# An attention and feed-forward kernel: the head's loads in 2 KB packets, its mask on VectorE, and the scores by chunks of keys

## The chip, the cores and the metric

The kernel runs on one core of a Trainium2 chip. The metric is the device time of one execution in microseconds (us); lower is better. The kernel was already tuned: TensorE is busy for 98% of the time, and a change of one microsecond is a third of a per cent. Executions of the same kernel spread over about 1 us.

## The reference

```python
# q, k, v: 8 batches x 8 heads x 576 positions x 64; w_in 512x2048, w_out 2048x512
scores = scale * np.matmul(q, k.transpose(0, 1, 3, 2))
mask = np.abs(pos[:, None] - pos[None, :]) <= 32          # a band
scores = np.where(mask, scores, -1000000000.0)
attn = softmax(scores)                                    # (max taken off, divided by the sum)
x = np.matmul(attn, v)            # -> 4608 tokens x 512
h = x @ w_in
g = h * (1.0 / (1.0 + np.exp(-1.702 * h)))
out = g @ w_out
```

## The kernel before

The tokens of all batches go through in 36 units of 128 keys. A unit has scores (TensorE), exponential (ScalarE), the band mask, values (TensorE), a normalisation (VectorE) and a transpose of x (TensorE in the head, by DMA later). Two units give 256 tokens for layer 1 and layer 2 of the feed-forward part, which fill TensorE. One call of `layer1`, eight matmuls, is called a layer-1 block here. The change touches the head, that is, the time before TensorE is in that dense part, and the scores.

In the head, the first batch comes in two parts: positions 0 to 320 ("A") and 320 to 576 ("B"). In part B, four neighbouring positions of one head are one piece of 1 KB in float32. Two heads are first copied side by side ("pairing", on VectorE), then transposed together:

```python
self.span = {"A": (0, 320), "B": (320, 256)}
...
def pair_heads(self, c, i, hp, eng, src=None):
    ...
    self.cast(eng, self.stage[c, i, "c"][:n, hp], src.rearrange("p h (j d) -> p j h d", j=JT))
...
def head(self):
    ...
    self.setup_neg()                    # triangles of -30000, five operations on GpSimd
    for m in range(3):
        self.load_v(m)                  # GpSimd issues these loads
    for c in "kq":
        self.load_heads("B", c)
    self.load_w_in(0)
    self.load_v(3)
    self.load_v(4, 0)
    for c in range(1, 4):
        self.load_w_in(c)
    ...
    for hp in range(4):
        self.pair_heads("k", "B", hp, dve)
    for hp in range(3):
        self.pair_heads("q", "B", hp, dve)
    for hp in range(4):
        if hp == 2:
            self.blind_again(3, 0)
        self.rows_T("k", "B", hp, "htho"[hp], dve)      # transposes, then a copy out of PSUM
        if hp == 0:
            self.pair_heads("q", "B", 3, dve)
        self.rows_T("q", "B", hp, "hoth"[hp], act)
    self.scores(2)
    self.scores(3)
    self.odd_v(2, dve)
    self.odd_v(3, dve)
    self.layer1(0, 0)
    self.values(2)
    self.norm(2)
    self.layer1(0, 1)
    self.values(3)
    self.norm(3)
    self.x_T(2, "t")
    ...
```

`blind(u)` writes the triangles of -30000 into the PSUM bank of the scores (PSUM is where this kernel's matmuls write) by a matmul with the identity, so that the first units need no mask afterwards. `odd_v` makes, on VectorE, a second copy of a v tile (`vo`) that is shifted by half a tile. `keep_busy` runs matmuls on zeros ("fillers", named junk in the profile). The scores of a unit were 32 matmuls of 64 keys by 64 queries:

```python
for hp in range(4):
    for blk in range(2):
        k0, q0 = (128 * u + 64 * blk) % RING, (128 * u + 64 * blk + 32) % RING
        for half in range(2):
            lo, at = 64 * half, k0 + 64 * (half ^ blk)
            for eo in range(2):
                r = slice(eo * 64, eo * 64 + 64)
                nc.tensor.matmul(sc[eo][lo:lo + 64, 2 * hp + blk, :], self.kT[r, hp, at:at + 64],
                                 self.qT[r, hp, q0:q0 + SQ], ...)
```

The softmax here doesn't subtract the row's maximum and nothing guards it: scores larger than these inputs give would overflow.

## Time and profile before

| | before |
|---|---|
| time, median of the first three executions | 293.69 us (293.09 to 294.04) |
| span of the profiled execution | 291.3 us |
| part B's queries land | 15.15 us |
| their scores start | 17.22 us |
| first layer-1 block starts | 18.25 us |
| second quarter of w_in lands | 21.18 us |
| third layer-1 block starts (needs that quarter) | 21.23 us |
| last matmul starts | 287.66 us |

All but the first two rows are times from the span's start. The prediction below shows the page's lines, the chain of the head and the transfers. This is VectorE's timeline; the bracket is the idle time ahead and what ended it.

```profile
13.73 1.17 DVE L105 COPY kc<-ks 64x512 bf16<-64x512 bf16 x4
15.17 0.69 DVE L105 COPY qc<-qs 64x512 bf16<-64x512 bf16 x3 [0.27 <-DMA qs<-in_q_dram]
```

The chain of waits goes through the 7.28 us of that query load. But VectorE had been pairing keys until 0.27 us before its first query copy. Had the queries come earlier, it would have been ready for them only 0.27 us sooner.

### The profile page before, as it was taken

Reading aid. Unit: us, or ns where it says so; the run is one execution under the profiler, and the core shown is the slowest. Engines: PE = TensorE matmul, PEld = TensorE weight load, DVE = VectorE, ACT = ScalarE, POOL = GpSimd, SP = SyncE. Lnnn points to the kernel's source line nnn. Section 1 sums busy time; section 2 is a strip of 40 time slices with the busy share of each in tenths; the row PEclk is TensorE's granted clock in tenths of the full one; section 3 lists DMA queues with packets and bytes.
Section 4 is the critical chain, followed back from the end, with each engine's and each line's share of the span. In section 5 each row is a group of like instructions: output and inputs, shape, how many; then the busy total and the mean of one; then the engine's idle time right before and its main releaser. Section 6 shows DMA issues by size and latency. Waiting matters only on the chain.

```text
span 291.3 us, 9542 instructions
## 1 busy us (share of the span) xinstructions
PE 285.4 (98%) x4021; PEld 234.7 (81%) x4021; DVE 188.7 (65%) x556; ACT 185.0 (64%) x306; POOL 102.1 (35%) x142
## 2 busy tenths in 40 slices
PE   7999999999999999999999999999999999999995
PEld 2569765866888888888888888888888888888884
DVE  3682477678575858585858585858585858583353
ACT  4677547685766767676767676767575757575330
POOL 8945534999536442543433434332000000000000
PEclk9999999999999999999999999999999999999999
DMA  9999999999999999999999999999915330303012
GB/s 149 156 191 206 199 186 178 168 136 154 159 136 189 137 158 156 146 145 158 161 154 164 184 103 150 142 178 115 183 36 144 39 99 13 100 13 100 2 72 72
DMA packets 145291, 38.83 MB, mean 133 GB/s; under 512 B 129888, under 2 KB 140896, under 8 KB 145248
## 3 DMA queue, kind: packets, MB, share of 16 engines
q0 software_dynamic: 97696, 18.16, 88.6%
q1 hardware_dynamic: 47104, 19.67, 41.0%
q8 instruction: 31, 0.51, 0.8%
q10 hardware_dynamic: 448, 0.39, 0.5%
q14 instruction: 12, 0.10, 0.1%
HBM read 36.96 MB, written 9.44 MB: 159 GB/s over the span
## 4 chain that ended last, share of the span: by engine, by line
PE 92%; DMA 2%; POOL 2%; DVE 1%; issue 0%; ACT 0%; POOLq 0%; DVEq 0%
PE h_ps L319 43%; PE o_ps L381 32%; PE o_ps L331 7%; PE sc L251 4%; PE pv L279 4%; DMA qs<-in_q_dram 2%; PE tp L179 1%; POOL ve L160 1%; PE tp L306 0%; POOL ks L137 0%; DVE qc L105 0%; DVE o_sb L399 0%; POOL neg L219 0%; DVE kT L105 0%; POOL qs L137 0%
## 5 line engine op out<-in xcount | busy, mean ns | idle before, releaser
L319 PE MATMUL h_ps<-xT,w_in_sb 128*128 128x256 bf16 x1152 | 135.1, 273 | 0.0
L321 ACT ACTIVATE g<-h_ps 128x512 f16<-128x512 f32 x144 | 85.5, 595 | 73.4 <-PE h_ps L319 72.1
L319 PEld LDWEIGHTS <-w_in_sb 128*128 128x128 bf16 x1152 | 112.0, 98 | 13.4
L160 POOL DMA_DIRECT2D ve<-in_v_dram x40 | 34.2, 859 | 76.5 <-PE pv L279 62.9
L381 PEld LDWEIGHTS <-gs 128*128 128x128 f16 x480 | 45.8, 98 | 5.8
L381 PE MATMUL o_ps<-w_sum,gs 128*128 128x256 f16 x360 | 44.3, 273 | 0.0
L257 ACT ACTIVATE p<-sc 128x512 bf16<-128x512 f32 x72 | 37.2, 604 | 2.7 <-PE sc L251 2.5
L381 PEld LDWEIGHTS <-g 128*128 128x128 f16 x360 | 34.1, 98 | 4.6 <-ACT g L321 0.2
L358 DVE TENSOR_TENSOR gs<-g 128x512 f16<-128x512 f16 x30 | 12.7, 425 | 38.1 <-ACT g L321 38.1
L291 DVE TENSOR_TENSOR x<-pv,rec 128x256 bf16<-128x256 f32 x72 | 30.6, 425 | 2.5
L381 PE MATMUL o_ps<-w_out_sb,g 128*128 128x256 f16 x240 | 29.0, 273 | 0.0
L105 DVE COPY part<-o_ps 128x256 f32<-128x256 f32 x45 | 19.1, 424 | 12.7 <-PE o_ps L381 11.6
L399 DVE TENSOR_TENSOR o_sb<-o_ps,part 128x256 f32<-128x256 f32 x45 | 19.0, 422 | 12.0 <-PE o_ps L381 11.4
L268 DVE TENSOR_TENSOR p<-p,mask 128x512 bf16<-128x512 bf16 x64 | 24.5, 424 | 0.7 <-ACT p L257 0.7
L147 POOL DMA_DIRECT2D qs<-in_q_dram x27 | 23.0, 873 | 4.7 <-DMA ks<-in_k_dram 2.9
L105 DVE COPY vo<-ve 64x528 bf16<-64x528 bf16 x69 | 21.8, 316 | 3.8 <-DMA ve<-in_v_dram 2.3
L147 POOL DMA_DIRECT2D ks<-in_k_dram x27 | 22.7, 856 | 3.9 <-DMA ks<-in_k_dram 1.8
L331 PE MATMUL o_ps<-w_out_sb,g 128*128 128x512 f16 x96 | 23.2, 380 | 0.0
L418 ACT ACT_TABLE_LOAD x15 | 19.2, 1283 | 0.3
L257 ACT ACT_TABLE_LOAD x15 | 19.2, 1283 | 0.3
L290 DVE RECIPROCAL rec<-pv 128x4 f32<-128x4 f32 x72 | 12.6, 175 | 8.3 <-PE pv L279 8.1
L279 PEld LDWEIGHTS <-p 128*64 128x64 bf16 x576 | 11.2, 110 | 5.9 <-DVE p L268 3.6
(71 smaller groups left out, 243.3 us busy)
## 6 DMA issues: line engine op xcount, KB each, us to landing
out_dram<-o_sb SPq DMA_DIRECT2D x34, 256.0 KB, 4.5
ve<-in_v_dram POOLq DMA_DIRECT2D x32, 128.0 KB, 6.8
ks<-in_k_dram POOLq DMA_DIRECT2D x22, 128.0 KB, 10.0
qs<-in_q_dram POOLq DMA_DIRECT2D x22, 128.0 KB, 12.1
w_in_sb<-in_moe_w_in_dram POOLq DMA_DIRECT2D x4, 512.0 KB, 11.2
w_out_sb<-in_moe_w_out_dram POOLq DMA_DIRECT2D x4, 512.0 KB, 15.1
ve<-in_v_dram POOLq DMA_DIRECT2D x8, 64.0 KB, 6.7
ks<-in_k_dram POOLq DMA_DIRECT2D x7, 64.0 KB, 5.5
```

Of the source, the lines that this page charges most:

```text
L105: (eng.copy if eng is self.nc.scalar else eng.tensor_copy)(out, in_)
L147: self.nc.gpsimd.dma_start(self.stage[key][off:off + m, n], src[b, :, s:s + m, :].rearrange("h s d -> s h d"))
L160: self.nc.gpsimd.dma_start(self.ve[m % NV][off:off + n, :, :self.D], self.v[b, :, s:s + n, :].rearrange("h s d -> s h d"))
L257: nc.scalar.activation(p[:, eo], sc[eo], AF.Exp, scale=self.scale)
L268: self.nc.vector.tensor_mul(pv, pv, msk.to_broadcast([128, 4, 2, SQ]))
L279: nc.tensor.matmul(acc[half][blk * 64:blk * 64 + 64, hh, :], p[:, h % 2, h // 2 * 2 + blk, :], vt[:, h, :D + 1], start=(hh == 0), stop=(hh ...
L291: nc.vector.tensor_mul(x[:, hs, :], acc[half][:, :, :D], rec[:, hs, :].to_broadcast([128, 4, D]))
L319: nc.tensor.matmul(hps[:, i, :], self.w_in_sb[:, kr, ff * 128:(ff + 1) * 128], self.xT[t][:, kr, :], start=(i == 0 and kr == 0), stop=(i = ...
L321: nc.scalar.activation(self.g[t][:, ffs[0]:ffs[1] + 1:ffs[1] - ffs[0], :], hps, AF.Gelu_apprx_sigmoid)
L331: nc.tensor.matmul(o_ps, self.g[t][:, ff, s * 128:(s + 1) * 128], self.w_out_sb[:, ff, :], start=(ff == 0), stop=(ff == self.NFF - 1))
L381: nc.tensor.matmul(self.part[t, key], x, y, start=(first and k == 0), stop=(k == 7), skip_group_check=True)
L418: self.nc.scalar.activation(self.spark, self.spark, AF.Gelu_apprx_sigmoid)
```

## The change

The intent is to start the dense part earlier: issue the loads sooner (mask off GpSimd), land the queries sooner (2 KB pieces, half a v tile behind the first weights), and get from landing to scores without pairing copies (64 small transposes, and for each of keys and queries two copies "side by side" on VectorE and ScalarE). The scores of a unit become 24 matmuls, by three chunks of keys of which the middle one meets 128 queries. Both first layer-1 blocks now come ahead of both value units. Twelve fillers become seven.

```diff
+    def load_rest(self, c):
+        ...
+        for g in range(2):
+            self.nc.gpsimd.dma_start(rest[32 * g:32 * g + 32],
+                                     src[0, 4 * g:4 * g + 4, 320:576, :].rearrange("h (p j) d -> p h (j d)", j=8))
+
+    def rest_T(self, c, kind, engs):
+        tp = self.bank(kind, [128, 2, 8, 64], BF16, "tp")
+        for n in range(4):
+            for j in range(8):
+                self.nc.tensor.transpose(tp[64 * (n % 2):64 * (n % 2) + 64, n // 2, j, :],
+                                         self.stage[c, "B"][:64, n, j * self.D:(j + 1) * self.D], self.ident[:64, :64])
+        ...
+        for g in range(2):
+            self.cast(engs[g], dst[:, 2 * g:2 * g + 2, 320:576].rearrange("r h (p j) -> r h p j", j=8),
+                      tp[:, :, :, 32 * g:32 * g + 32].rearrange("r h j p -> r h p j"))
...
# setup_neg: one memset and four selects on GpSimd become 14 small VectorE operations
...
         for hp in range(4):
-            for blk in range(2): ...                     # 8 matmuls of 64x64 per hp, as above
+            for chunks in ((1, 0), (2,)):                # 6 matmuls per hp
+                for eo in range(2):
+                    r = slice(eo * 64, eo * 64 + 64)
+                    for c in chunks:
+                        lo = 64 * (c % 2)
+                        b0, n = (1, 1) if c == 2 else (0, 1 + c)
+                        nc.tensor.matmul(sc[eo][lo:lo + 64, 2 * hp + b0:2 * hp + b0 + n, :],
+                                         self.kT[r, hp, k0 + 64 * c:k0 + 64 * c + 64],
+                                         self.qT[r, hp, q0 + SQ * b0:q0 + SQ * (b0 + n)], ...)
...
-        for m in range(3):
+        for m in range(2):
             self.load_v(m)
-        for c in "kq":
-            self.load_heads("B", c)
+        self.load_v(2, 0, 64)
+        for c in "kq":
+            self.load_rest(c)
         self.load_w_in(0)
+        self.load_v(2, 64)
...
         self.blind(2)
+        self.rest_T("k", "t", (act, dve))
+        self.x_T(0, "h", act)
+        self.x_T(1, "h", act)
+        self.rest_T("q", "o", (dve, act))
         self.blind(3)
-        (pairing copies, 32 transposes of pairs, eight copies)
+        self.keep_busy(2, "h")
         self.scores(2)
         self.scores(3)
...
         self.layer1(0, 0)
+        self.layer1(0, 1)
         self.values(2)
         self.norm(2)
-        self.layer1(0, 1)
         self.values(3)
```

More of the change, by code (lines that the diff above doesn't have):

```diff
@@ L55, in __init__ @@
         self.stage, self.paired = {}, set()
-        self.span = {"A": (0, 320), "B": (320, 256)}
+        self.span = {"A": (0, 320)}
         self.xT, self.g, self.o_ps = {}, {}, {}
@@ L155, in rows_X, with load_v @@
                                              self.stage[c, i][:, n].rearrange("p h d -> p (h d)"))
-    def load_v(self, m, half=None):
-        for i, (off, b, s, n) in enumerate(self.pieces(128 * m, 128)):
-            if half in (None, i):
-                self.nc.gpsimd.dma_start(self.ve[m % NV][off:off + n, :, :self.D],
-                                         self.v[b, :, s:s + n, :].rearrange("h s d -> s h d"))
+    def load_v(self, m, lo=0, hi=128):
+        for off, b, s, n in self.pieces(128 * m + lo, hi - lo):
+            self.nc.gpsimd.dma_start(self.ve[m % NV][lo + off:lo + off + n, :, :self.D],
+                                     self.v[b, :, s:s + n, :].rearrange("h s d -> s h d"))
     def odd_v(self, m, eng):
@@ L191, in rows_T @@
                   tp[:, :, :size // JT].rearrange("r j p -> r p j"))
+    def load_rest(self, c):
+        rest = self.stage[c, "B"] = self.work.tile([128, 4, 8 * self.D], BF16, name=c + "s", tag=c + "s", bufs=3)
+        src = {"q": self.q, "k": self.k}[c]
+        for g in range(2):
[7 more added lines that the diff above has]
+                                         self.stage[c, "B"][:64, n, j * self.D:(j + 1) * self.D], self.ident[:64, :64])
+        dst = {"q": self.qT, "k": self.kT}[c]
+        for g in range(2):
+            self.cast(engs[g], dst[:, 2 * g:2 * g + 2, 320:576].rearrange("r h (p j) -> r h p j", j=8),
+                      tp[:, :, :, 32 * g:32 * g + 32].rearrange("r h j p -> r h p j"))
     def load_raw(self, c, hp, eng):
@@ L210, in setup_neg @@
     def setup_neg(self):
-        pool = self.nc.gpsimd
+        dve, pad = self.nc.vector, SQ // 2
+        lo, hi = slice(0, 64), slice(64, 128)
         self.neg = self.cst.tile([128, 2, SQ], BF16, name="neg")
-        pool.memset(self.neg, 0.0)
-        for b in range(2):
-            for half in range(2):
-                sign = 1 if half == b else -1
-                ap = self.neg[64 * half:64 * half + 64, b, :]
-                pool.affine_select(out=ap, in_=ap, compare_op=ALU.is_ge, fill=-30000.0, base=0,
-                                   pattern=[[-sign, SQ]], channel_multiplier=sign)
-    def blind_again(self, u, eo):
-        neg = self.neg.rearrange("k (o b) s -> k o b s", o=1).to_broadcast([128, 4, 2, SQ])
-        self.nc.tensor.matmul(self.sc[u][eo].rearrange("k (h b) s -> k h b s", b=2), self.ident, neg,
-                              start=True, stop=False, skip_group_check=True)
+        tri = [self.cst.tile([128, pad + SQ], BF16, name=f"tri{i}") for i in range(2)]
+        for i in range(2):
+            dve.memset(tri[i][:, :pad], 0.0)
+        for rows in (lo, hi):
+            dve.tensor_copy(tri[0][rows, pad:], self.ident[rows, rows])
+        for i in range(6):
+            a, b = tri[i % 2], tri[(i + 1) % 2]
+            dve.tensor_add(b[:, pad:], a[:, pad:], a[:, pad - (1 << i):pad + SQ - (1 << i)])
+        for rows, b in ((lo, 0), (hi, 1)):
+            dve.tensor_scalar(out=self.neg[rows, b, :], in0=tri[0][rows, pad - 1:pad + SQ - 1], scalar1=-30000.0,
+                              scalar2=None, op0=ALU.mult)
+            dve.tensor_scalar(out=self.neg[rows, 1 - b, :], in0=tri[0][rows, pad:], scalar1=30000.0, scalar2=-30000.0,
+                              op0=ALU.mult, op1=ALU.add)
     def blind(self, u):
@@ L241, in scores @@
         sc = self.sc.pop(u)
-        n = 0
+        k0, q0 = 128 * u % RING, (128 * u + 32) % RING
         for hp in range(4):
-            for blk in range(2):
-                k0 = (128 * u + 64 * blk) % RING
-                q0 = (128 * u + 64 * blk + 32) % RING
-                for half in range(2):
-                    lo, at = 64 * half, k0 + 64 * (half ^ blk)
-                    for eo in range(2):
-                        r = slice(eo * 64, eo * 64 + 64)
-                        nc.tensor.matmul(sc[eo][lo:lo + 64, 2 * hp + blk, :], self.kT[r, hp, at:at + 64],
-                                         self.qT[r, hp, q0:q0 + SQ], start=(seen and n == 0),
-                                         stop=(n == 7), skip_group_check=not seen)
-                n += 1
+            for chunks in ((1, 0), (2,)):
[6 more added lines that the diff above has]
+                                         self.kT[r, hp, k0 + 64 * c:k0 + 64 * c + 64],
+                                         self.qT[r, hp, q0 + SQ * b0:q0 + SQ * (b0 + n)],
+                                         start=(seen and hp == 0 and c < 2), stop=(hp == 3 and c > 0),
+                                         skip_group_check=not seen)
         p = self.work.tile([128, 2, 8, SQ], BF16, name="p", tag="p", bufs=5)
@@ L436, in head @@
         self.setup_neg()
-        for m in range(3):
+        for m in range(2):
             self.load_v(m)
+        self.load_v(2, 0, 64)
         for c in "kq":
-            self.load_heads("B", c)
+            self.load_rest(c)
         self.load_w_in(0)
+        self.load_v(2, 64)
         self.load_v(3)
-        self.load_v(4, 0)
+        self.load_v(4, 0, 64)
         for c in range(1, 4):
@@ L452, in head @@
         self.load_w_out(1)
-        self.load_v(4, 1)
+        self.load_v(4, 64)
         for m in range(5, 7):
@@ L471, in head @@
         self.odd_v(0, dve)
-        self.odd_v(1, act)
+        self.odd_v(1, dve)
         self.keep_busy(3, "h")
@@ L475, in head @@
         self.norm(0)
-        self.keep_busy(3, "o")
-        self.x_T(0, "t", act)
-        self.keep_busy(1, "o")
+        self.keep_busy(2, "o")
         self.values(1, "oa")
         self.norm(1)
-        self.keep_busy(4, "a")
-        self.x_T(1, "a", act)
         self.blind(2)
+        self.rest_T("k", "t", (act, dve))
+        self.x_T(0, "h", act)
+        self.x_T(1, "h", act)
+        self.rest_T("q", "o", (dve, act))
         self.blind(3)
-        self.keep_busy(1, "h")
-        for hp in range(4):
-            self.pair_heads("k", "B", hp, dve)
-        for hp in range(3):
-            self.pair_heads("q", "B", hp, dve)
-        for hp in range(4):
-            if hp == 2:
-                self.blind_again(3, 0)
-            self.rows_T("k", "B", hp, "htho"[hp], dve)
-            if hp == 0:
-                self.pair_heads("q", "B", 3, dve)
-            self.rows_T("q", "B", hp, "hoth"[hp], act)
+        self.keep_busy(2, "h")
         self.scores(2)
```

## The prediction

> **What bounds the kernel now.** I read the page first, then the chain of waits of the first 24 us, the DMA issues with their landings, and the timelines of GpSimd and TensorE there.
>
> ```profile
> PE 285.4 (98%) x4021; PEld 234.7 (81%) x4021; DVE 188.7 (65%) x556; ACT 185.0 (64%) x306; POOL 102.1 (35%) x142
> PE 92%; DMA 2%; POOL 2%; DVE 1%; issue 0%; ACT 0%; POOLq 0%; DVEq 0%
> ```
>
> TensorE carries 92% of the chain that ended last; everything else on it is the head. So two things can shorten the kernel: less TensorE work in the dense part, or an earlier start of it. The chain of waits shows the head (start, length, what):
>
> ```profile
> 4.37 2.85 POOL ve L160 x3
> 7.21 0.66 POOL ks L137
> 7.87 7.28 DMA qs<-in_q_dram
> 15.15 0.02 issue
> 15.17 0.69 DVE qc L105 x3
> 15.86 0.33 DVE kT L105
> ...
> 17.29 0.48 PE sc L251 x24
> 17.77 0.02 issue
> 17.79 0.53 PE sc L251 x40
> 18.32 0.98 PE h_ps L319 x8
> 19.30 0.38 PE pv L279 x16
> ```
>
> The second part of the first batch's queries is issued at 7.87 us and lands at 15.15. From there 2.07 us of copies and transposes lead to the scores at 17.22 in TensorE's timeline, and the first layer-1 block follows at 18.25. After that TensorE has no visible gap. But there is a second limit close behind. In GpSimd's timeline the second quarter of w_in is issued at 10.88, and the DMA view of that moment gives its time to landing (last column):
>
> ```profile
> 10.88 2.27 POOL L109 DMA_DIRECT2D w_in_sb<-in_moe_w_in_dram  x3
> w_in_sb<-in_moe_w_in_dram POOLq DMA_DIRECT2D x1, 512.0 KB, 10.3
> ```
>
> 10.88 + 10.3 is 21.2 us. The first block that needs that quarter is the third layer-1 block, and in TensorE's timeline it starts at 21.23:
>
> ```profile
> 21.23 1.05 PE L319 MATMUL h_ps<-xT,w_in_sb 128*128 128x256 bf16 x8
> ```
>
> So queries and weights are limits of almost equal length. If only the queries came earlier, TensorE would stand before this weight quarter instead. Later weights have room: the third quarter of w_in lands near 23.8 and is needed near 26.7.
>
> **What the Trainium skill says.** (1) "PSUM — Partial Sum Buffer", section "PSUM bank collisions raise a hardware error": two engines must not touch one bank and quadrant at once, reads against reads included, and ACT against DVE is made to wait as well. Each of the change's two copies "side by side" reads all 128 partitions of one 2 KB bank. In the built program's order the VectorE copy of the keys waits for ScalarE's, and ScalarE's copy of the queries waits for VectorE's. So I take them as one after the other; before, no such pair exists, so the trace can't show it. (2) "DMA: Bandwidth & Descriptors", section "Why small descriptors are slow (HBM only)": a fixed cost per packet and descriptor. The trace agrees: the old loads (512 packets with 1 KB read each) land 1.97 us apart, k at 7.20 + 6.0 = 13.2, q at 7.87 + 7.3 = 15.17; the first w_in quarter (512 packets with 2 KB read) lands 2.2 us later (8.54 + 8.8 = 17.3). Twice the bytes cost little more than the same number of packets. (3) "TensorE: Matmul & The Clock Gate", section "What's actually happening": the array's clock halves after an idle window of about 3.4 us. In the trace the first eight fillers take 3.55 us, 0.44 each, and three later ones 0.82 us together, so a gap that is too long would show.
>
> **The change part by part.**
>
> *Mask on VectorE.* GpSimd loses one memset and four selects, 2.97 to 4.32 us in its timeline: 1.35 us before the first v load. VectorE gains about 14 small operations in a chain. It sits idle 3.01 us until 4.43, waiting for the raw keys; at an estimated 0.13 us each (between its 72 ns memsets and 0.175 us reciprocals) that is 1.8 us and hidden. How much of GpSimd's 1.35 us reaches the landings? The v loads land 4.1 us after their issue at 4.32 and 5.3, about 0.97 apart, as the issues do, so they are partly limited by issue; but the loads ahead of them land only at 2.34 + 5.0 = 7.34. I count 0.3 us.
>
> *Half of a v tile behind the first w_in quarter.* The third v tile lands at about 11.35, 1.95 after the second. Half of it moved: 0.5 to 1.0 us for the queries, nothing for the second w_in quarter, which still comes after it.
>
> *2 KB packets.* Keys and queries go from 512 packets each to 256 of double size. By the w_in row, 256 such packets cost half of 2.2 to 2.55 us (the quarters of w_in land about 2.5 us apart later), so 1.1 to 1.3 us instead of about 1.9: 0.6 to 0.8 each, 1.2 to 1.6 for both. I take 1.2. This shifts everything behind, the weights too.
>
> Queries: 15.15 - 0.3 - 0.7 - 1.2 gives about 12.9. Second w_in quarter: 21.2 - 0.3 - 1.2 gives about 19.7.
>
> *From the queries' landing to the scores.* The pairing copies go (eight of 0.29 us on VectorE). Instead 32 transposes of 64 columns (one per 16 ns by the old 64-column pairs: 0.5 us, with latency 0.7), then two copies of 128x512 with a strided side. Today's rows for this form are 0.69 us on VectorE and 0.585 on ScalarE. One after the other with semaphores: 0.7 + 0.69 + 0.59 + 0.1, about 2.1 us. That is the 2.07 of before: truly parallel copies would have given 1.5. The first half of the first score unit can start after the first copy, which gains another 0.3 or so. Scores would end at 12.9 + 2.1 + 0.6, about 15.6 instead of 18.25.
>
> *Order behind the scores.* Two layer-1 blocks (0.98 each) to 17.6, then both value units (0.38 each) one after the other, to 18.4. The transposes of the first unit wait for its normalisation, two pairs of 0.18 + 0.42 us on VectorE, until about 19.1: a new stall of about 0.7 us, since a layer-1 block no longer lies between. TensorE is at the third layer-1 block at about 19.3. The weights are there at 19.7. So the weights end it: 21.2 - 19.7, a gain of 1.5 us.
>
> *Scores by key chunks.* Matmuls per unit go from 32 to 24, with the same columns. Does the count or the columns cost? The chain of waits has both kinds near each other:
>
> ```profile
> 46.77 0.38 PE pv L279 x16
> 47.15 0.38 PE sc L251 x32
> ```
>
> 16 value matmuls run two at a time, 32 scores four at a time: eight rounds each, of 64 or 65 columns, and the same 0.38 us. Rounds cost, not instructions. In the new order each head pair still sends chunks 0 and 2, 64 columns each, through the same quarter of the array, while chunk 1 with 128 columns runs beside them: eight rounds per unit again. I count 0.1 us over all 36 units, and at the very most 1 us.
>
> *Fillers.* Twelve fall to seven. All stand in times of waiting; not on the path.
>
> Sum: 1.5 + 0.1, about 1.6; I take off 0.1 for friction. 293.7 - 1.5 = 292.2 us.
>
> **The rivals.** First, the head gains its full shift of the queries, about 2.5 us, and the weights keep up: against it speaks the landing at 21.2 beside the use at 21.23. It would give 291.2. Second, the landing hardly moves: transfers of the same bytes are already at the rate of the memory, and the packets were not the cost. For it speaks that larger loads later run 1 KB reads nearly as fast (the 448 KB k load has 896 packets and lands 15.6 us after issue, in a full queue). Then only the half v tile is left, the weights do not move, and the time stays at 293.3. Third, the new stall at the transposes and serial copies, perhaps a halved clock with five fillers gone, eat it up: about 293.5 to 294. Fourth, fewer score matmuls do pay, if issue and weight loads bound them (24 for 32, a quarter of 0.25 us over 36 units, 2.3 us at most): 290. The equality of the two 0.38 us rows speaks against it.
>
> **Range and chances.** The first two rivals give 291.2 and 293.3, and runs of before spread over 0.95 us. Eight times in ten I expect 291.0 to 293.5. A change of 2% would be 5.9 us; the head has at most some 4 us to give, and no part adds as much. So within 2%: 0.97, faster 0.02, slower 0.01.
>
> **What would show it.** Right: the queries land near 12.9 us; the scores end near 15.6; TensorE waits for VectorE before the transposes after the first two layer-1 blocks; the third layer-1 block starts with the landing of the second w_in quarter, near 19.7; a steady score unit still costs 0.38 us in the chain, and the distance from that block to the end is unchanged. Wrong: a score burst that is clearly shorter (fourth rival), queries landing after 14 us (second), the two copies from one bank overlapping in time, or fillers and transposes at twice their length before the scores (the clock).

## The result, and the profile after

| | before | after | predicted |
|---|---|---|---|
| time, median of 4 executions each, us | 293.47 | 291.61 | 292.2 |
| ratio (95% interval) | | 0.9941 (0.9915 to 0.9967) | |
| part B's queries land, us | 15.15 | 12.74 | 12.9 |
| scores of part B start / first layer-1 block starts, us | 17.22 / 18.25 | 15.42 / 16.37 | – / 15.6 |
| second w_in quarter lands, us | 21.18 | 19.49 | 19.7 |
| third layer-1 block starts, us | 21.23 | 19.95 | 19.7 |
| last matmul starts, us | 287.66 | 285.89 | – |

Ratios here are the mean time of one kernel's fast runs over that of the other's of the same rounds, so they are not quite the ratio of the medians quoted. Repeated later on another chip (the last experiment), the changed kernel gave 0.9985 (0.9964 to 1.0006): the two sets put the gain at 0.6% and at 0.15%, and the second alone can't be told from no gain.

The profiled executions differ by 1.77 us at the last matmul. 1.28 us of that are there at the third layer-1 block; 0.49 come later. The page of the changed kernel, busy times and the chain by engine:

```profile
PE 282.7 (98%) x3757; PEld 233.5 (81%) x3759; DVE 192.0 (66%) x562; ACT 183.7 (63%) x302; POOL 101.8 (35%) x140
PE 94%; DMA 2%; DVE 1%; ACT 1%; issue 0%; ACTq 0%; DVEq 0%
```

TensorE has 264 matmuls fewer and is busy 2.7 us less. The chain still is TensorE's; the 2% of GpSimd on it are gone. The chain of waits through the head, after (start, length, what):

```profile
12.27 0.82 PE tp L205 x32
13.09 0.55 PE tp L326 x8
13.64 0.84 PE tp L205 x32
...
14.51 0.70 DVE qT L105
...
15.23 0.59 ACT qT L105
...
15.87 0.57 PE sc L270 x25
16.44 1.85 PE h_ps L339 x16
18.29 0.27 PE pv L299 x8
...
18.58 0.19 DVE rec L310
...
18.80 0.42 DVE x L311
19.23 0.10 DVE rec L310
...
19.35 0.43 DVE x L311
...
19.83 0.28 PE tp L326 x2
```

Three things are to be seen. No transfer stands on it: the queries land at 12.74, but TensorE comes to their transposes only at 13.64, behind the keys' transposes (12.27) and those of x (13.09). The two copies of the queries follow one another (VectorE 14.51, ScalarE 15.23), as predicted. And the third layer-1 block is held by the normalisation, from 18.56 to 19.83; the weights had been there since 19.49. For those, the lines of GpSimd's timeline and of the transfers after:

```profile
11.15 2.27 POOL L109 DMA_DIRECT2D w_in_sb<-in_moe_w_in_dram  x3
w_in_sb<-in_moe_w_in_dram POOLq DMA_DIRECT2D x1, 512.0 KB, 8.3
```

The second quarter is issued 0.27 us later than before (11.15 against 10.88) and yet lands 1.7 us earlier, for it takes 8.3 us instead of 10.3; probably less is ahead of it in the queue by then, since more had been moved before. These are the windows of 9 to 12 us of before, then after; the last number is GB/s moved, and the five pairs are the busy times of TensorE, its weight loads, VectorE, ScalarE and GpSimd:

```profile
9.00:12.00 3.00, 2.74 (x39) 1.12 (x27) 1.41 (x5) 2.95 (x6) 3.00 (x5) 1.00 1.38 143
```

```profile
9.00:12.00 3.00, 2.83 (x68) 1.48 (x56) 2.79 (x10) 2.07 (x4) 2.60 (x5) 1.00 1.25 202
```

143 GB/s become 202. In the dense part, a pair of score units in the chain, before and then after:

```profile
107.58 0.67 PE sc L251 x64
```

```profile
106.11 0.63 PE sc L270 x32
```

A pair costs 0.04 us less (the count at the end is of the matmuls that the chain goes through, of 64 and 48). A unit by itself, further up in both chains, still takes 0.38 us.

### The profile page after: what moved, and what is told of

It reads as the page before. It is cut to its first block, busy times and chain, and to the rows that moved or that the text cites.

```text
span 289.8 us, 9009 instructions
## 1 busy us (share of the span) xinstructions
PE 282.7 (98%) x3757; PEld 233.5 (81%) x3759; DVE 192.0 (66%) x562; ACT 183.7 (63%) x302; POOL 101.8 (35%) x140
## 4 chain that ended last, share of the span: by engine, by line
PE 94%; DMA 2%; DVE 1%; ACT 1%; issue 0%; ACTq 0%; DVEq 0%
PE h_ps L339 43%; PE o_ps L401 32%; PE o_ps L351 7%; PE pv L299 4%; PE sc L270 4%; DMA q_raw<-in_q_dram 2%; PE tp L178 1%; PE tp L326 1%; PE tp L205 1%; ACT qT L105 0%; ACT p L277 0%; PE sc L253 0%; DVE x L311 0%; DVE o_sb L419 0%; DVE qT L105 0%
## 5 line engine op out<-in xcount | busy, mean ns | idle before, releaser
L105 DVE COPY vo<-ve 64x528 bf16<-64x528 bf16 x71 | 24.5, 345 | 4.7 <-DMA ve<-in_v_dram 3.1
L105 DVE COPY part<-o_ps 128x256 f32<-128x256 f32 x45 | 19.1, 423 | 12.4 <-PE o_ps L401 11.4
```

The source lines that it names most:

```text
L105: (eng.copy if eng is self.nc.scalar else eng.tensor_copy)(out, in_)
```

## The experiments

The theory after the result: the loads gain from the mask, the half tile and the packets together, the pairing copies no longer stand behind them, and the steady scores give up to half a microsecond. The rivals: one of these parts gives it all, or the new stall and the serial copies keep back a gain that a small repair would release. The experiments came in three sets of four, each set on one chip with its own runs of the kernel before (medians 293.40, 293.26 and 292.97). All twelve gave the right result.

**1. The old score matmuls in the changed kernel.**

```diff
-            for chunks in ((1, 0), (2,)): ...      # 24 matmuls per unit
+            for blk in range(2): ...               # the old 32 per unit
```

> The changed kernel with the score matmuls of before (32 per unit instead of 24), nothing else. Theory: fewer instructions pay only where two units stand together (bursts of 64): 0.67 us for such a pair instead of 0.63, some 14 pairs, so about 0.5 us longer than the changed kernel, near 292.1; the third layer-1 block still starts at 19.9 to 20.0. Rival (the prediction's 0.1 us): 291.7, and the 0.04 us per pair come from something else in the changed kernel, so the pairs stay at 0.63.

Measured: 293.31 us, ratio 1.0003 (0.9970 to 1.0036). The whole gain is gone, although the queries landed at 12.92 and the second weight quarter at 20.35. Its chain of waits shows why:

```profile
13.65 0.52 PE tp L205 x18
14.16 0.94 issue
15.10 0.51 PE tp L205 x14
...
19.45 0.60 PE pv L299 x29
20.05 1.22 issue
21.27 0.22 PE pv L299 x3
```

"issue" is time in which the engine waited for nothing that the profile shows. TensorE stops for 0.94 us in the middle of 32 equal transposes, whose data had been there for 1.2 us, and for 1.22 us within the value matmuls. The first pause falls after matmul 220 of TensorE's recorded order, the second after matmul 346. In the changed kernel (runs 7 and 12 show it best, with 0.44 and 0.22 us) a pause after the same matmul (221 in traces that have one more record before it) falls behind the second blind, in time that TensorE spends waiting for the copies anyway. Sixteen more score matmuls ahead of it, eight in each of the first two units, move it into the transposes. Between the two pauses lie 127 weight loads, as many matmuls (one has no record) and two semaphore instructions: 256 instructions.

The traces also show what the pauses end with. One DMA queue moves instructions, in packets of 16 KB. Its line on the page of this run, then of the changed kernel (packets, MB, share):

```profile
q8 instruction: 32, 0.52, 0.8%
```

```profile
q8 instruction: 29, 0.48, 0.7%
```

It has three packets more where TensorE has 288 matmuls more. The times of its first packets are read from the traces:

| | packet starts, us | packet ends, us | TensorE goes on, us | from the packet's end, us |
|---|---|---|---|---|
| run 1, first pause | 12.70 | 13.64 | 15.10 | 1.46 |
| run 1, second pause | 18.82 | 19.76 | 21.27 | 1.51 |
| run 6 | 12.46 | 13.83 | 15.40 | 1.57 |
| run 10 | 13.22 | 14.25 | 15.67 | 1.42 |

Runs 7, 8 and 12 have 1.44, 1.49 and 1.44 us. So TensorE goes on 1.4 to 1.6 us after such a packet in all seven pauses, also where the packet took longer (run 6) or came later (run 10). The kernel before reaches its matmul 220 only at 17.3 us, long after its packet (12.02 to 13.17), and doesn't stop there. That TensorE waits in these pauses for its next instructions fits all of this; no run moved a packet by itself, so it isn't proved by experiment.

**2. The new score matmuls alone in the kernel before.** (The edit is the score part of the diff above.)

> The kernel before with the new score matmuls alone. Theory: the head is as before (third layer-1 block at 21.2, queries at 15.1), pairs of units take 0.63 instead of 0.67 us, and the time is about 0.5 us under before: 293.0. Rival (0.1 us): 293.4. If issue bound all scores, each unit would fall from 0.38 too, and the time by over 1 us.

Measured: 293.01 us, 0.9986 (0.9949 to 1.0023), not told apart from nothing. The scores of the dense part did take 0.66 us less, but layer 2 and the values took 0.9 us more (see run 7). The trace was worth more than the time. In this run the unchanged loads landed the queries at 13.83, 1.3 us before those of the first profile, and the weights at 20.53. Yet the scores started at 17.39, not earlier than 17.22. The chain:

```profile
13.66 0.42 DVE x L291
14.08 1.06 DVE kc L105 x4
15.14 0.41 DVE qc L105 x2
```

No transfer is on it: VectorE's normalisation of the second unit, then its pairing copies, hold the old head. So landings vary by more than a microsecond between runs of the same loads, and in the old head an earlier landing buys next to nothing.

**3. 1 KB packets in the changed kernel.**

```diff
-        for g in range(2):
-            self.nc.gpsimd.dma_start(rest[32 * g:32 * g + 32],
-                                     src[0, 4 * g:4 * g + 4, 320:576, :].rearrange("h (p j) d -> p h (j d)", j=8))
+        self.nc.gpsimd.dma_start(rest[:64], src[0, :, 320:576, :].rearrange("h (p j) d -> p h (j d)", j=4))
...
```

> The changed kernel, but the second part of keys and queries loaded in 1 KB reads (one DMA of 512 packets each, 64 partitions), with the same number and size of transposes and copies. Theory (packets cost): queries land about 1.2 us later, near 13.9, the second w_in quarter too, near 20.7, so the third layer-1 block moves from 19.95 to about 20.7 and the time to about 292.4. Rival (bytes cost, not packets): queries near 13.0, the quarter by 19.7, and the block stays at 19.95, 291.6.

Measured: 292.08 us, 0.9957 (0.9929 to 0.9986). Against the first run of the changed kernel the queries land 0.26 us later (13.00), the second weight quarter 1.1 us later (20.62), and the third layer-1 block waits for it (20.66). Against run 1, which has the changed loads and ran on the same chip, it is only 0.08 and 0.27 us. So going back to 1 KB costs 0.1 to 0.3 us at the queries, not the 1.2 predicted, and 0.3 to 1.1 at the weights. The edit isn't packets alone, though: it also makes two issues of four, so GpSimd has issued the queries by 6.8 instead of 7.7 us, and yet they land later. What 2 KB packets would be worth with the issues kept in place wasn't tested.

**4. The mask back on GpSimd in the changed kernel.**

```diff
-        dve.memset(...); dve.tensor_copy(...); dve.tensor_add(...) x6; dve.tensor_scalar(...) x4
+        pool.memset(self.neg, 0.0)
+        pool.affine_select(...) x4
```

> The changed kernel with the mask built on GpSimd again. Theory: GpSimd issues the v loads 1.35 us later, but landings move only some 0.3 us, the queries come near 13.1 and still before TensorE is ready for them (13.57), and the raw loads land 0.2 us earlier, so the third layer-1 block stays within 0.2 us of 19.95: 291.6. Rival (the issue was the limit): queries 1 us or more later, near 13.9, second w_in quarter near 20.5, time 292.3.

Measured: 293.96 us, 1.0016 (0.9986 to 1.0047): the gain is gone. The v loads land as in the changed kernel (8.09 against 8.11), so at that point the 1.35 us of later issue cost nothing. Behind them they do: queries 13.51, first weight quarter 16.81, second 21.87, which is 0.6, 0.7 and 1.5 us behind run 1 on the same chip, and 0.8, 1.5 and 2.4 behind the first run of the changed kernel. The chain, and the window of 9 to 12 us:

```profile
12.01 9.86 DMA w_in_sb<-in_moe_w_in_dram
...
21.92 0.61 PE h_ps L332 x4
```

```profile
9.00:12.00 3.00, 2.83 (x68) 1.50 (x59) 2.52 (x10) 2.06 (x4) 3.00 (x5) 1.00 1.13 160
```

GpSimd is busy without a break, 160 GB/s are moved instead of 202, and the third layer-1 block stands until the weights land. The scores still start at 15.46, against 15.42: TensorE comes to the queries' transposes only at about 13.6 in any case. So the mask's place decides the weights, not the scores.

**5. The third v tile whole again, before the keys.**

```diff
-        self.load_v(2, 0, 64)
+        self.load_v(2)
...
-        self.load_v(2, 64)
```

> The changed kernel with the third v tile loaded whole, ahead of keys and queries. Theory: queries land 0.5 to 0.7 us later, near 13.3, still before TensorE gets to their transposes at 13.57; the second w_in quarter keeps its place; so no change: third layer-1 block at 19.9 to 20.0, 291.6. Rival (queries are still the limit): the block and the time 0.5 us later, 292.1.

Measured: 292.09 us, 0.9965 (0.9950 to 0.9980); queries at 12.65, third block at 19.74. No effect, where 0.7 us had been predicted for the queries: with half a tile they landed at 12.89 to 13.22 on the same chip (runs 6 to 8).

**6. Two PSUM banks for the copies.** Each copy gets a bank of its own, so that both can run together.

```diff
-        tp = self.bank(kind, [128, 2, 8, 64], BF16, "tp")
+        for b in range(2):
+            tp = self.bank(kinds[b], [128, 8, 64], BF16, "tp")
...
-            self.cast(engs[g], dst[:, 2 * g:2 * g + 2, 320:576]..., tp[:, :, :, 32 * g:32 * g + 32]...)
+            self.cast(engs[b], dst[:, b:b + 3:2, 320:576]..., tp...)
```

> The changed kernel with each pair of copies reading two PSUM banks (split by head pair), so that neither waits for the other. Theory (one bank made them serial): ScalarE and VectorE copies overlap in time, scores start near 15.1 and end about 0.7 us before 16.44; behind them the wait for the normalisation stays, so the third layer-1 block moves to where the second w_in quarter lands, about 19.5: 0.4 us gained, 291.2. Rival (ScalarE's own queue of four copies is the limit, not the bank): scores end less than 0.3 us earlier.

Measured: 292.73 us, 0.9973 (0.9942 to 1.0003). The copies do overlap now. VectorE's and ScalarE's timelines of this run:

```profile
14.27 0.69 DVE L105 COPY qT<-tp 128x512 bf16<-128x512 bf16 x1 [0.38 <-PE tp L207]
14.57 0.58 ACT L105 COPY qT<-tp 128x512 bf16<-128x512 bf16 x1
```

They end at 14.96 and 15.15, instead of 15.82 for the second one. This agrees with the dependency that the prediction took from the Trainium skill ("PSUM — Partial Sum Buffer", section "PSUM bank collisions raise a hardware error"): with one bank they ran one after the other. But the scores started at 15.92, not earlier than 15.42, since the fillers ahead of them ran only at 15.40: the pause of run 1 had become the last thing to end. What followed cost more, and is told under run 7.

**7. The transposes in alternating order.** Neighbouring transposes write different halves of the partitions.

```diff
-        for n in range(4):
-            for j in range(8):
+        for m, j in [(m, j) for m in range(2) for j in range(8)]:
+            for n in (2 * m, 2 * m + 1):
```

> The changed kernel with the 32 transposes in another order: output halves 0 to 63 and 64 to 127 alternate from one to the next. Theory (the prediction's 16 ns each was for alternating pairs): 32 transposes take 0.5 instead of 0.82 us; the copies behind the keys start 0.3 us earlier and with them everything to the scores: scores end near 16.1, the third layer-1 block near 19.65. Rival: 26 ns is the cost of such a transpose in any order, nothing changes.

Measured: 292.29 us, 0.9971 (0.9956 to 0.9986). Its chain:

```profile
13.54 0.62 PE tp L205 x32
14.16 0.54 PE sc L253 x2
14.70 0.44 issue
15.14 0.59 PE junk L444 x2
```

32 transposes take 0.62 instead of 0.82 us. The pause ends at 15.14 all the same, the fillers follow, and the scores start at 15.66. In runs 6 and 7 TensorE also loses time much later. TensorE's timeline of run 6 has a wait at 111 us, of 0.64 us, for the x that the DMA transposes:

```profile
111.67 1.03 PE L339 MATMUL h_ps<-xT,w_in_sb 128*128 128x256 bf16 x8 [0.64 <-DMA xT<-x]
```

And in runs 2 to 8 and 12 a value unit near 65 us starts late and stops, since VectorE's copies and masks come late; the chain of run 5:

```profile
63.05 0.51 issue
63.56 0.84 DVE vo L105
64.40 0.67 DVE p L288 x2
...
65.11 0.41 PE pv L299 x14
```

The changed kernel's first run had neither. To size this, I summed the times from each matmul's start to the next one's, from the ninth layer-1 block to the end, by kind. Scores take 10.99 to 11.19 us in the three kernels with the old form (before, 1 and 9), and 10.52 to 10.54 in the eleven with the new one, so 0.5 to 0.7 us less in each. Layer-2 matmuls, unchanged, take 113.47 us in before, 113.67 in the first run after, 114.21 in run 7 and 114.49 in run 6, and the values 10.42 or 10.72. Up to 1.3 us are thus given back. An earlier TensorE is not enough to explain it, for run 2 gives back 0.9 us with its third layer-1 block at 21.35. Near 65 us it goes with VectorE: the six `odd_v` copies just before take 4.65 to 4.84 us in all in the eight runs that stop there, 4.18 in the first run after, and 2.1 to 2.4 in before and in runs 1, 9, 10 and 11. Why the same copies take twice as long wasn't tested.

**8. The old order behind the scores.** One layer-1 block stands again between the value units.

```diff
         self.layer1(0, 0)
-        self.layer1(0, 1)
         self.values(2)
         self.norm(2)
+        self.layer1(0, 1)
         self.values(3)
```

> The changed kernel with the second layer-1 block between the two value units, as before. Theory: the wait of 1.27 us for the normalisation before the first transposes of x falls to under 0.4; the value unit waits somewhat for v (VectorE's odd copy, near 17.3), and the third layer-1 block starts near 19.6: 291.3. Rival (the v tiles are the limit in this order): the first value unit waits until after 17.9 and the block starts at 20.0 or later.

Measured: 291.62 us, 0.9947 (0.9932 to 0.9962). The wait for the normalisation is gone; the chain now reads:

```profile
11.45 8.58 DMA w_in_sb<-in_moe_w_in_dram
...
20.08 1.05 PE h_ps L339 x8
```

The weights, here at 20.03, hold the block instead. The two limits lie within a few tenths of each other, and which one ends the wait is decided by that run's landing.

**9. The mask on VectorE alone, in the kernel before.** (The edit is run 4's the other way round, made to the kernel before.)

> The kernel before with the mask built on VectorE, nothing else. Theory (GpSimd's issue, not the DMA engines, is the limit from 6 to 12 us, so its 1.35 us carry through): moved bytes from 9 to 12 us rise from 125 to 154 GB/s to about 170 to 200, queries land near 13.6 to 14, the second w_in quarter near 20, and the third layer-1 block starts near 20.2 instead of 21.2: time about 292.5. Rival (the prediction's 0.3 us): queries near 14.8, block at 20.9, 293.2.

Measured: 293.46 us, 1.0017 (1.0004 to 1.0030), if anything slower, and neither expectation. The queries landed at 14.62 and the second weight quarter at 20.27, 0.5 and 0.9 us earlier than in the first profile, but the scores started at 17.97. Its chain is that of run 2 again: VectorE's normalisation until 14.66, then four pairing copies of keys in 1.08 us and two of queries in 0.41. That holds the old head. It was also later by some 0.6 us than in run 2, and the chain goes back to the first part's queries of heads 4 to 8, which landed at 8.20 in this run, against 7.34 in before.

**10. The new scores with 16 more matmuls ahead.** One filler becomes 17 small matmuls, to move the pause without touching the scores.

```diff
-        self.keep_busy(2, "o")
+        self.keep_busy(1, "o")
+        self.keep_small(17, "o")        # 17 matmuls of 64x32 on zeros
```

> The changed kernel with one filler of 512 columns replaced by 17 small ones of 32 columns, in the wait ahead of the second value unit: 32 more TensorE instructions before the queries' transposes, no more work. Theory (the run with old scores lost its gain because TensorE ran out of instructions: two pauses without any wait, after matmul 220 and after matmul 346 in its order): the same pauses of about 1 us after the same matmul numbers, so inside the queries' transposes and at the end of the value units; third layer-1 block at 21 to 21.7, time near 293.2. Rival (the old scores themselves cost it): at most 0.2 us later than the changed kernel, third block by 20.2, 291.8.

Measured: 292.72 us, 0.9997 (0.9984 to 1.0010). The test is not clean: the small matmuls took 0.70 us, and the keys' transposes came at 13.00 instead of 12.27. But the pause came back, at the same place in TensorE's order, in the chain:

```profile
14.38 0.52 PE tp L205 x18
14.90 0.77 issue
15.67 0.51 PE tp L205 x14
```

Eighteen transposes, then 0.77 us of nothing, as in run 1, now with the new scores. So it is the number of matmuls ahead, not their form, that puts the pause there. The third layer-1 block started at 21.65, as in run 1 (21.66). The second pause of run 1 did not appear.

**11. The repairs together.** Two banks, alternating transposes, no fillers behind the queries, the old order behind the scores, and the second weight quarter in two halves. (The edits of runs 6, 7 and 8 are not shown again.)

```diff
-        for c in range(1, 4):
+        for c in (2, 3):
+            self.load_w_in(c, 8)
+        for c in (2, 3):
             self.load_w_in(c)
...
-        self.keep_busy(2, "h")
```

> Changed kernel with two banks, alternating transposes, no fillers behind the queries, the second layer-1 block back between the value units, and the second w_in quarter loaded in two halves, so that the third layer-1 block waits for the first half alone. Theory: scores start when the instructions are there, near 15.2, end near 15.8; the third block starts near 19.2, 0.7 us before the changed kernel. Then the second batch's queries come next: they were paired just 0.25 us before TensorE used them, so no more than 0.3 to 0.4 us may remain: 291.3. Rival: the freed TensorE meets nothing else and the full 0.7 us stay, 290.9; or the clock falls for lack of fillers, 292 or more.

Measured: 292.07 us, 0.9968 (0.9956 to 0.9981), five executions. The scores start at 15.07 and the third layer-1 block at 19.14, 0.8 us before the changed kernel in run 12 on the same chip. At the last matmul 0.13 us are left of it (285.98 against 286.11). TensorE's timeline, then the chain, of this run:

```profile
35.76 0.40 PE L178 MATMUL tp<-ident,qc 128*128 128x128 bf16 x4 [0.30 <-DVE qc L105]
```

```profile
33.51 10.93 DMA ve<-in_v_dram
44.46 0.04 DVE vo L105
...
45.47 0.41 PE pv L299 x14
```

The second batch's queries land at 35.31 (35.44 in the first run after), and a v tile at 44.44; TensorE, being earlier, now waits for both. In this run the next loads took the head's place as the limit.

**12. The changed kernel again, unchanged.**

> The changed kernel itself once more, on the same chip as the last three, as a measure for them: 291.6, third layer-1 block at 19.7 to 20.1, no pause of TensorE inside the queries' transposes; the second w_in quarter may land anywhere from 19.1 to 20.1, as in its variants.

Measured: 292.21 us (291.67 to 293.75), 0.9985 (0.9964 to 1.0006). The profiled execution is that of 291.67, and has the first run's milestones: queries 12.97, third block 19.93, last matmul 286.11. Two of six executions took 293.56 and 293.75, at granted clocks of 0.994 and 0.999; they weren't profiled, and what held them stays open.

## Why the prediction was right or wrong, point by point

The time (292.2, measured 291.61 and 292.21) and the range were right. So were both landings, to 0.2 us, the copies that follow one another, and the new stall at the normalisation. Several steps that made the sum were not, so that the time came out is partly luck: the third layer-1 block came 0.25 us later than predicted (19.95 for 19.7), and the rest of the kernel gave 0.49 us instead of 0.1. The landings were lucky too: over the runs with these loads the queries landed at 12.74 to 13.37 and the quarter at 19.1 to 20.7.

- **"The weights end it."** This is the step that failed in the profiled run. The normalisation ended the wait (19.83), 0.3 us after the weights (19.49). Run 8 shows that taking it away only hands the wait to the weights. The prediction had the stall end at 19.1; it is later because the scores ended near 16.4, not 15.6.
- **From landing to scores.** Two terms. The transposes were sized at 16 ns each; in this order they take 26 ns (0.82 us for 32), and even in alternating order 19 (0.62). And the queries' transposes were taken to start at the landing, but 0.9 us of other TensorE work stood ahead. Hence run 4 and run 3 moved the landing by up to 0.8 us without moving the scores.
- **What bounds the kernel now.** "Queries and weights" left out a third limit of the same length: VectorE's normalisation and pairing. Runs 2 and 9 show it. The removal of the pairing copies was booked at zero, "the 2.07 of before", but without it the earlier landing would have bought 0.27 us at most. This is inferred from before and runs 2 and 9: no run has the new loads with the old pairing.
- **Mask: 0.3 us.** Mis-sized. Its place costs 0.6 to 0.8 us at the queries and 1.5 to 2.4 at the weights; without it the gain is gone (run 4). Alone it isn't enough either (run 9).
- **Packets: 1.2 us, half a v tile: 0.7 us.** Each taken back alone costs the queries at most 0.3 us (run 3, with fewer issues besides) or nothing (run 5). Yet the landing came out right. With neither of the two the queries landed at 14.62 (run 9), with one at 13.00 or 12.65, with both at 12.74 to 13.37: it looks as if either one were enough. These runs are of three chips and the landings scatter, so how the 1.6 us split between them stays open.
- **Scores by chunks: 0.1 us.** Mis-sized, and the fourth rival was partly right. The dense part's scores take 0.5 to 0.7 us less, in the pairs (0.67 to 0.63), while the single unit stays at 0.38. What the kernel keeps of it differs from run to run: from the third layer-1 block to the last matmul the first run after took 0.49 us less than before, run 12 0.25 less, and run 2 0.2 more. In the head they count for more: with the old form the changed kernel isn't faster than before at all, mostly because of the two pauses (run 1; its weights, at 20.35, alone would have cost 0.4 us of the 1.7 us by which its third layer-1 block is late).
- **Second and third rivals.** The landing did move, and no halved clock was seen: the granted clock of the head's windows was 1.00. The third was right that the gain can be eaten up, but by the pauses of run 1 and by later waits, which the prediction didn't foresee.

## What to carry to other kernels

When a wait on the chain is long but the engine behind it had only just finished something else, the second limit is that engine: look at its idle time before the wait's end (0.27 us here) before counting on an earlier transfer. A head has several limits of nearly equal length, so single reversals of a combined change can each cost all of it (mask, scores) or nothing (v tile), and a gain of under a microsecond may be met again by the next loads. When an engine stops in the middle of equal instructions with no wait in the profile, count the instructions up to the pause: one that stays at the same number while the time moves points to the instruction stream. Then look for the packets of the instruction queue just before; the order or number of instructions ahead decides whether it falls in time that is idle anyway.

## What the Trainium skill lacked or had wrong

- "Runtime: NRT & Kernel Launch", section "Instruction fetch mechanics", says that instructions are refilled in blocks of 256 and that the cost of crossing into the next block is "mostly hidden". Here TensorE paused for 0.94 and 1.22 us (run 1) and 0.77 us (run 10) with no wait shown, run 1's two pauses 256 instructions apart, and went on 1.4 to 1.6 us after a packet of the instruction queue had ended. If these are refills, they aren't hidden in a head that is short of time. The page "Advanced Engine Details and Errata", section "ISA Cache", gives the line of 256 instructions and no cost.
- "DMA: Bandwidth & Descriptors", section "Anatomy of one DMA — SWDGE (gpsimd) path", calls descriptor generation small and variable and says "You can emit a lot of descriptors before the incremental cost shows up". Here GpSimd took 2.49 us to issue two v tiles and a half, and with the 1.35 us mask ahead of the loads (run 4) it was busy without a break, the rate from 9 to 12 us was 160 GB/s instead of 202, and a weight quarter landed 1.5 to 2.4 us later. So the time of issue can count. It doesn't always: in run 9 the keys were issued 1.6 us earlier than before (5.61 for 7.20) and landed at the same time (13.15 for 13.19).
- The same page, section "Why small descriptors are slow (HBM only)", works its overhead out for a descriptor of 256 bytes and gives no cost of a whole load. Here the queries in packets of 1 KB landed 0.1 to 0.3 us later than in packets of 2 KB, though GpSimd had issued them 0.9 us earlier (run 3).
- "TensorE: Matmul & The Clock Gate", the parts on packing small matmuls and on transposes, has a figure for a 128x128 transpose and none for small ones. 32 of 64 columns took 0.82 us when neighbours wrote the same half of the partitions, and 0.62 us when they alternated (run 7).
